# Longer DMA runs for keys, wq and values, with a set-aside quarter, in a decode step of attention and a gated feed-forward layer

## The chip, the cores and the metric

The kernel runs on 1 core of one Trainium2 chip. A core has five engines that run side by side: TensorE (PE) for matrix products, VectorE (DVE), ScalarE (ACT), GpSimd (POOL), and SyncE (SP), which here only issues transfers. Sixteen DMA engines move data from memory (HBM) into the on-chip buffers. The metric is device time in microseconds (us), lower is better. Before the change it is 696.13 us, the median of 3 runs (696.13 to 696.16).

## The reference

One token (x, 512 numbers) goes through an attention block with a long cache and through a gated feed-forward layer; a scalar gate mixes the two results.

```python
def _A_ref(x, k_cache, v_cache, wq, wo):       # Hq, Dh = 32, 128; 8 KV heads, Sk = 32768
    q = (x @ wq).reshape(B, Sq, Hq, Dh).transpose(0, 2, 1, 3)
    k, v = jnp.repeat(k_cache, 4, axis=1), jnp.repeat(v_cache, 4, axis=1)
    p = softmax(einsum("bhqd,bhkd->bhqk", q, k) * Dh ** -0.5)
    o = einsum("bhqk,bhkd->bhqd", p, v)
    return o.transpose(0, 2, 1, 3).reshape(B, Sq, Hq * Dh) @ wo

def _B_ref(x, w1, w3, w2):                     # D, F = 512, 1792
    return (silu(x @ w1) * (x @ w3)) @ w2

g = sigmoid((x * gate_w).sum(-1, keepdims=True))
return g * _A_ref(...) + (1 - g) * _B_ref(...)
```

All is float32. The keys are 134 MB, the values as many; wq and wo have 8.4 MB each, w1, w2 and w3 3.7 MB each: 296 MB in all, each byte read once.

## The kernel before

**Tiles and units.** Two tiles of 64 KB in each of the 128 partitions, `big_a` and `big_b`, take turns for nearly everything that is loaded. Each has two halves, `region(b, z)`, with the dependency names A0, A1, B0, B1. A *key unit* t (0 to 15) is 8.4 MB: a quarter of the keys of a pair of KV heads. It comes as two loads, one per half (`load_keys`, L331), and in each of them a partition gets a run of 32 KB. A *value unit* s (0 to 15) is half a head's values, 8.4 MB; units 0 to 11 come as one load with runs of 64 KB into `big_b` (`load_values`, L409). The values lag the keys by four units (`LAG`).

**What is done with a unit.** For each half of a key unit DVE makes four chunks: a block transpose of 128x2048 into `kt0` or `kt1` in turn (L355). PE multiplies each chunk with a small window of queries (L344; ScalarE copies the window into `winc`, L338) and adds up in PSUM. Behind the eighth chunk ScalarE copies the scores out (L361) and PE clears the bank (L244). After each fourth unit PE turns the scores (`turn`, L374, instructions on L371), and DVE with ScalarE makes the softmax of that pair (L378: maximum L381, subtraction L393, exponent L398, sums L403). A value unit is multiplied by its weights in 32 products (`values_all`, L430, with the weights copied by ScalarE on L418), and DVE takes the useful blocks out (`own`, L440, with L442 and L446).

**Order.** The instruction order of every engine is the order in which the program adds operations; each engine works through its list and waits on semaphores. SyncE has one list of loads, each of which waits until the readers of its target are done. The semaphore on which a transpose tells that it is done is counted down by the PE product that uses it, so a load that overwrites keys waits for PE's product on the last chunk read from its half. In the loop over units (L453) a step adds: scores of unit t, the next keys' loads, and for t of 4 and more the value product of unit t - 4, then the next values' load. The softmax of four units stands one unit later, behind the scores of unit t + 1, and `turn` at the end of the step t = 3, 7, 11, 15. PE's part of this is written as three nested loops (L661 to L676), with a branch that leaves out the values in the first four units.

**Start.** SyncE loads wq in two halves into `big_a` (x between them), then w1 and w3 into `big_b`, then keys 0 into `big_a`, keys 1 into `big_b`, 2 into a, 3 into b, and all later keys into a. PE makes the queries (L270), ScalarE and DVE lay them into `win` (L288 to L298); then come the hidden products of w1 and w3 (L307), the sigmoid (L313) and three DVE steps (L314, L316, L320).

**End.** Values 12 (two halves), wo (quarters of 2.1 MB in `wo_t`, a tile that nothing else uses), 13, 14 (two halves) and 15 (in three pieces), then w2 in five pieces into `big_a`. DVE multiplies wo's rows into `acc` (`mix`, L525); the last products close the sum and ScalarE's queue writes 2 KB out.

Of the kernel before, what the change touches and what calls it, by code (L numbers as in the profile page):

```python
# [116 lines left out]
def kernel(  # L117
# [79 lines left out]
    wqd = wq.rearrange("(p c) n -> p (c n)", c=NC)  # L197
    for z in range(2):
        load(region(0, z), wqd[:, z * R:(z + 1) * R], [f"A{z}"])
        if z == 0:  # L200
            load(rows[0][0:1, :], x.rearrange("a b n -> (a b) n"), ["row0"])
            pr.add("ACT", lambda: nc.scalar.dma_start(rows[1][0:1, :], gate_w.rearrange("(o n) -> o n", o=1)),
                   writes=["row1"], inc="gate", by=16)
    for z, t in enumerate((w1, w3)):
        load(region(1, z)[:, 0:NC * F], t.rearrange("(p c) f -> p (c f)", c=NC), [f"B{z}"])
# [6 lines left out]
    mt, mtt = sbuf("mt", 32), sbuf("mtt", 32)  # L212
# [47 lines left out]
    pe(columns, reads=["row0", "ident"], writes=["m0"])  # L260
# [3 lines left out]
    for c in range(NC):  # L264
        def part(c=c):
            t = region(0, c // 2)
            for b in range(2):
                for j in range(4):
                    o = ((c % 2) * HKV + 4 * b + j) * REP * DH
                    ins = T.matmul(  # L270
                        pf[b][32 * j:32 * j + 32, :], xp[:, c, :], t[:, o:o + REP * DH],
                        start=(c == 0), stop=(c == NC - 1),
                    )
            return ins
        pe(part, reads=[f"A{c // 2}", "xp"], writes=["f0", "f1"])
# [25 lines left out]
    for z in range(2):  # L301
        def ff(z=z):
            t = region(1, z)
            for c in range(NC):
                for j in range(4):
                    o = c * F + FJ * j
                    ins = T.matmul(  # L307
                        pf[2 + z][32 * j:32 * j + 32, 0:FJ], xp[:, c, :], t[:, o:o + FJ],
                        start=(c == 0), stop=(c == NC - 1),
                    )  # L310
            return ins
        pe(ff, reads=[f"B{z}", "xp"], writes=[f"f{2 + z}"])
    act(lambda: A.activation(silu[:, 0:FJ], pf[2][:, 0:FJ], AF.Sigmoid), reads=["f2"], writes=["silu0"])  # L313
    dve(lambda: V.tensor_mul(silu[:, 0:FJ], silu[:, 0:FJ], pf[2][:, 0:FJ]), reads=["f2", "silu0"], writes=["tmp0"])  # L314

    dve(lambda: V.scalar_tensor_tensor(  # L316
        rows[0][:, 0:FJ].rearrange("p (k a) -> p k a", k=FR), silu[:, 0:FJ].rearrange("p (a k) -> p k a", k=FR),
        gate[:, 1:2], pf[3][:, 0:FJ].rearrange("p (a k) -> p k a", k=FR), op0=ALU.mult, op1=ALU.mult,
    ), reads=["tmp0", "gate1", "f3"], writes=["row0"])
    dve(lambda: V.transpose(htp.rearrange("p k a -> p (k a)"), rows[0][:, 0:FJ]), reads=["row0"], writes=["htp"])  # L320

    kd = k_cache.rearrange("a (w u) s d -> w (a u s d)", u=2).rearrange("w (p m z r) -> w m z p r", p=P, m=4, z=2)
    vd = v_cache.rearrange("a h (e p n) d -> (a h) e p (n d)", e=2, p=P)

    def where(t):
        return 1 if t in (1, 3) else 0

    def load_keys(t):  # L331
        b = where(t)
        for z in range(2):
            load(region(b, z), kd[t // 4, t % 4, z], ["AB"[b] + str(z)])
# [15 lines left out]
    def scores(t, z, win_op):  # L350
        kin = region(where(t), z).rearrange("p (n c j) -> p c n j", c=4, j=32)
        key = "AB"[where(t)] + str(z)
        for c in range(4):
            dst = kt[c % 2].rearrange("p (n i) -> p n i", i=32)
            k = dve(lambda c=c, d=dst: V.transpose(d, kin[:, c]), reads=[key], writes=[f"kt{c % 2}"], credit="keys")  # L355
# [18 lines left out]
    def turn():  # L374
        for f in range(4):
            pe(lambda f=f: turn_part(f), reads=[("sb", m) for m in range(4)] + ["ident"], writes=[f"f{f}"], loop=True)

    def softmax(w):  # L378
# [17 lines left out]
        ), reads=["top"], writes=banks)  # L396
        for u in range(2):
# [4 lines left out]
            ), reads=banks, writes=[("prob", u)])  # L402
# [46 lines left out]

    load_keys(0)  # L450
    vals = {}
    first = window(0, 0)
    for t in range(NH):  # L453
        v = t - LAG
        scores(t, 0, first)
        second = window(t, 1)
        if v >= 1:
            own(v - 1)
            if v % 4:
                vals[v] = (vals[v], weights(v))  # L460
        scores(t, 1, second)
        scores_out(t)
        if t + 1 < NH:
            load_keys(t + 1)
            first = window(t + 1, 0)

        if v >= 0 and v % 4 == 0:
            softmax(v // 4)
            vals[v] = (vals[v], weights(v))
        if v >= 0:  # L470
            values_loop(*vals.pop(v))
        if v + 1 >= 0 and t + 1 < NH:
            vals[v + 1] = load_values(v + 1)
        if t % 4 == 3:
            turn()
# [83 lines left out]
    def load_halves(s):  # L559
        for z in range(2):  # L560
            load(region(0, z), vd[s // 2, s % 2][:, z * R:z * R + R], [f"A{z}"])

    load_halves(12)
    load_wo(0)
    load(big[1], vd[6, 1], ["B0", "B1"])
    own(11)
    softmax(3)
# [7 lines left out]
    load_halves(14)  # L575
# [59 lines left out]
    for a, b in parts[2:]:  # L635
        ff_down([(htp[:, k, :], w2t[:, k, :], k == 8, k == FR - 1) for k in range(a, b)], reads=["htp", ("w2", a)])
        if a == 8:
# [4 lines left out]
           reads=["res"], inc="out", by=16)  # L642
# [5 lines left out]
    a = next(i for i, o in enumerate(ops) if o.loop)  # L648
    b = max(i for i, o in enumerate(ops) if o.loop) + 1
    assert all(o.loop for o in ops[a:b])  # L650
    pr.emit("PE", ops[:a])
    half = T.alloc_register("half")
    T.reg_mov(half, 0)
# [5 lines left out]


    with nc.Fori(0, NP, 1, engines=[PE], head_slot={PE: 0}):  # L661
# [46 lines left out]
```

## Time and profile before

| | |
|---|---|
| median of the runs | 696.13 us |
| the profiled execution: its time, its span | 695.86 us, 694.0 us |
| granted TensorE clock, mean | 0.774 |
| PE, DVE, ACT busy | 402.1, 376.2, 45.3 us |
| bytes read from HBM, mean rate | 296.23 MB, 427 GB/s |
| L355, 128 transposes of 128x2048 | 2287 ns each |
| L344, 1024 products of scores | 186.1 us in all |
| L430, 768 products of values | 110.2 us in all |

The span goes from the first to the last instruction of the program. "Busy" counts neither waiting nor issuing. A page cuts the span into 40 equal slices and gives each one's busy share in tenths. A line of the timeline has the start, the length, engine, line and operation, the tiles written and read, how many instructions are taken together, and in brackets how long the engine had been idle and what ended that. In the waits, a line has the total time, the number of waits and the longest. "PEq" is PE's sequencer, "SPq" SyncE's.

### The profile page before, as it was taken

How to read it: one execution, taken by the hardware profiler on the slowest of the kernel's cores; microseconds unless marked ns; L12 is line 12 of the kernel's file. 1: busy time of each engine (PE TensorE's matmuls, PEld its weight loads, DVE VectorE, ACT ScalarE, POOL GpSimd, SP SyncE). 2: the span in 40 equal slices, each digit the busy share in tenths (PEclk: the TensorE clock that was granted, in tenths of full speed). 3: DMA queues.
4: the chain of work that ended last, by engine and by line, in shares of the span. 5: the costliest groups of instructions: out<-in, count | busy, mean ns of one | idle time of the engine just before them, and what ended most of it. 6: DMA issues, size and time to landing. Idle time of an engine off the chain costs nothing. (4 is left out here: it accounts for less than half of the span.)

```text
span 694.0 us, 5676 instructions
## 1 busy us (share of the span) xinstructions
PE 402.1 (58%) x2400; PEld 92.6 (13%) x2400; DVE 376.2 (54%) x263; ACT 45.3 (7%) x90; POOL 2.6 (0%) x15
## 2 busy tenths in 40 slices
PE   3636566647556554746667644538456555376756
PEld 1100001101010110201010101201010101131112
DVE  1029999885719081686619091786529090654121
ACT  0200000020100000010100000020100000100000
POOL 1000000000000000000000000000000000000000
PEclk9966877877887796867665898977876776777679
DMA  9999999999999999999999999999999999999996
GB/s 391 421 425 444 431 425 433 467 399 427 451 419 431 444 448 404 450 423 427 465 406 448 416 442 419 442 431 450 427 423 434 419 472 399 447 425 424 427 422 285
DMA packets 9380, 296.34 MB, mean 427 GB/s; under 512 B 1046, under 2 KB 1050, under 8 KB 1436
## 3 DMA queue, kind: packets, MB, share of 16 engines
q1 hardware_dynamic: 9362, 296.23, 99.2%
q8 instruction: 5, 0.08, 0.0%
q14 instruction: 3, 0.02, 0.0%
q10 hardware_dynamic: 10, 0.00, 0.0%
HBM read 296.23 MB, written 0.00 MB: 427 GB/s over the span
## 5 line engine op out<-in xcount | busy, mean ns | idle before, releaser
L355 DVE STREAM_TRANSPOSE kt<-big_a 128x2048 f32<-128x2048 f32 x112 | 250.2, 2287 | 182.3 <-DMA big_a<-in_A_k_cache_dram 180.8
L344 PE MATMUL ps<-kt,winc 128*32 128x512 f32 x1024 | 186.1, 807 | 132.7 <-PEq L658 132.7
L430 PE MATMUL ps<-big_b,pv 128*32 128x512 f32 x768 | 110.2, 738 | 74.0 <-PEq L658 74.0
L344 PEld LDWEIGHTS ps<-kt,winc 128*32 128x32 f32 x1024 | 26.5, 122 | 287.0 <-issue 287.0
L430 PEld LDWEIGHTS ps<-big_b,pv 128*32 128x32 f32 x768 | 30.3, 132 | 153.7 <-issue 153.7
L355 DVE STREAM_TRANSPOSE kt<-big_b 128x2048 f32<-128x2048 f32 x16 | 35.7, 2287 | 3.2 <-DMA big_b<-in_A_k_cache_dram 3.2
L527 DVE SCALAR_TENSOR_TENSOR acc<-wo_t,own_rows,acc 128x512 f32<-128x512 f32 x24 | 18.0, 752 | 28.2 <-DMA wo_t<-in_A_wo_dram 27.4
L244 PE MATMUL ps<-acc 128*128 128x512 f32 x34 | 20.5, 687 | 21.8 <-PEq L658 20.3
L338 ACT COPY winc<-win 128x128 f32<-128x128 f32 x32 | 9.8, 307 | 341.9 <-PE ps L344 341.9
L540 PE MATMUL ps<-big_b,probs 128*32 128x512 f32 x128 | 19.4, 767 | 14.2 <-DMA big_b<-in_A_v_cache_dram 14.2
L361 ACT COPY sb<-ps 128x512 f32<-128x512 f32 x16 | 17.0, 1063 | 151.3 <-PE ps L344 151.3
L540 PE MATMUL ps<-big_a,probs 128*32 128x512 f32 x128 | 20.7, 811 | 5.1 <-DMA big_a<-in_A_v_cache_dram 5.1
L403 DVE TENSOR_REDUCE sums<-probs 128x8 f32<-128x2048 f32 x4 | 15.3, 3822 | 8.0 <-ACT probs L398 8.0
L442 DVE TENSOR_TENSOR tmp<-ps,own_b 128x512 f32<-128x512 f32 x12 | 7.9, 655 | 20.1 <-PE ps L430 20.1
L307 PE MATMUL turned<-big_b,xp 128*32 128x448 f32 x64 | 9.2, 734 | 9.6 <-DMA big_b<-in_B_w_dram 9.6
L270 PE MATMUL turned<-big_a,xp 128*32 128x512 f32 x64 | 11.7, 902 | 2.7 <-DMA big_a<-in_A_wq_dram 2.4
L446 DVE TENSOR_REDUCE red<-tmp 128x128 f32<-128x1024 f32 x6 | 11.5, 1915 | 0.2
L244 PEld LDWEIGHTS ps<-acc 128*128 128x128 f32 x34 | 5.4, 201 | 39.1 <-issue 37.6
L398 ACT ACTIVATE probs<-turned 128x1024 f32<-128x1024 f32 x8 | 7.8, 1021 | 38.5 <-DVE turned L393 38.5
L393 DVE TENSOR_TENSOR turned<-turned,top 128x2048 f32<-128x2048 f32 x4 | 9.2, 2300 | 0.1
L381 DVE TENSOR_REDUCE mt<-turned 128x8 f32<-128x2048 f32 x4 | 9.0, 2260 | 0.0
L549 DVE TENSOR_SCALAR red<-ps,own_b 128x128 f32<-128x128 f32 x2 | 0.7, 348 | 15.3 <-PE ps L540 15.3
(80 smaller groups left out, 95.7 us busy)
## 6 DMA issues: line engine op xcount, KB each, us to landing
big_a<-in_A_k_cache_dram SPq DMA_DIRECT2D x28, 4096.0 KB, 28.3
big_b<-in_A_k_cache_dram SPq DMA_DIRECT2D x4, 4096.0 KB, 30.7
big_a<-in_A_v_cache_dram SPq DMA_DIRECT2D x4, 4096.0 KB, 27.7
big_a<-in_A_wq_dram SPq DMA_DIRECT2D x2, 4096.0 KB, 16.4
wo_t<-in_A_wo_dram SPq DMA_DIRECT2D x4, 2048.0 KB, 18.0
big_b<-in_B_w_dram SPq DMA_DIRECT2D x2, 3584.0 KB, 33.7
big_b<-in_A_v_cache_dram SPq DMA_DIRECT2D x1, 4096.0 KB, 27.3
big_b<-in_A_v_cache_dram SPq DMA_DIRECT2D x2, 2048.0 KB, 34.0
```

Of the source, the lines that this page charges most:

```text
L244: return T.matmul(ps_s, acc[:, 0:P], acc, start=True, stop=False, skip_group_check=True)
L270: ins = T.matmul(pf[b][32 * j:32 * j + 32, :], xp[:, c, :], t[:, o:o + REP * DH], start=(c == 0), stop=(c == NC - 1),)
L307: ins = T.matmul(pf[2 + z][32 * j:32 * j + 32, 0:FJ], xp[:, c, :], t[:, o:o + FJ], start=(c == 0), stop=(c == NC - 1),)
L338: lambda: A.copy(winc, win[:, t // 4, :, 16 - 16 * z:48 - 16 * z]),
L344: ins = T.matmul(ps_s[32 * g:32 * g + 32, :], winc[:, c, :], kt[c % 2][:, 512 * g:512 * g + 512], start=False, stop=False, skip_group_chec ...
L355: k = dve(lambda c=c, d=dst: V.transpose(d, kin[:, c]), reads=[key], writes=[f"kt{c % 2}"], credit="keys")
L361: lambda: A.copy(sb[:, :, :, t % 4], ps_s.rearrange("p (n i) -> p n i", i=32)),
L403: dve(lambda: V.tensor_reduce(sums[:, 8 * w:8 * w + 8].rearrange("p (u q) -> p u q", u=2), probs[:, :, 0:1024].rearrange("p u (n q) -> p u ...
L430: ins = T.matmul(ps_o[32 * t:32 * t + 32, :], pv[:, o:o + 32], big[1][:, n * P:(n + 4) * P], start=((z, g) == (0, 0)), stop=((z, g) == (1, ...
L446: dve(lambda: V.tensor_reduce(red[h], tmp.rearrange("p e b d -> p d (e b)"), axis=AX.X, op=ALU.add), reads=["tmp0", "tmp1"], writes=[("red ...
L527: dve(lambda k=k: V.scalar_tensor_tensor(acc, wo_t[:, k, :], own_rows[:, w, k:k + 1], acc, op0=ALU.mult, op1=ALU.add,), reads=["wo", ("own ...
L540: ins = T.matmul(ps_o[32 * t:32 * t + 32, :], prob[u][:, o:o + 32], vt[:, n * P:(n + 4) * P], start=((e, z, g) == (0, 0, 0)), stop=((e, z, ...
```

## The change

Keys are loaded as one load per unit with runs of 64 KB, and so are wq and value units 12 and 14 (unit 15 stays in three pieces). As soon as a key unit has landed, ScalarE copies the quarter that the last two chunks of the second half need (128x4096) into `wo_t` (`set_aside`); those two transposes read it there, so the next load into the tile waits for six transposes and that copy. Key units 0 and 2 go to `big_b`, 1 and 3 to `big_a`. w1 and w3 are loaded behind key unit 3, into `big_b`, and the hidden products and the three DVE steps stand behind the fourth unit's `turn` and softmax; they use the PSUM banks `pm` in place of `pf`. x and gate_w are both issued by ScalarE. `turn` now stands ahead of the value product, and the softmax in the same step as `turn`. An instruction ahead of the exponent writes a one-column tile `mark`. PE has two loops, of 4 and of 12 units, with `turn` and the hidden products written out between them.

```diff
-    wqd = wq.rearrange("(p c) n -> p (c n)", c=NC)
-    for z in range(2):
-        load(region(0, z), wqd[:, z * R:(z + 1) * R], [f"A{z}"])
-        if z == 0:
-            load(rows[0][0:1, :], x.rearrange("a b n -> (a b) n"), ["row0"])
-            pr.add("ACT", lambda: nc.scalar.dma_start(rows[1][0:1, :], gate_w.rearrange("(o n) -> o n", o=1)),
-                   writes=["row1"], inc="gate", by=16)
-    for z, t in enumerate((w1, w3)):
-        load(region(1, z)[:, 0:NC * F], t.rearrange("(p c) f -> p (c f)", c=NC), [f"B{z}"])
+    for i, t in enumerate((x.rearrange("a b n -> (a b) n"), gate_w.rearrange("(o n) -> o n", o=1))):
+        pr.add("ACT", lambda i=i, t=t: nc.scalar.dma_start(rows[i][0:1, :], t), writes=[f"row{i}"], inc="row", by=16)
+    load(big[0], wq.rearrange("(p c) n -> p (c n)", c=NC), ["A0", "A1"])
...
-        pe(part, reads=[f"A{c // 2}", "xp"], writes=["f0", "f1"])
+        pe(part, reads=["A0", "A1", "xp"], writes=["f0", "f1"])
...
-    kd = k_cache.rearrange("a (w u) s d -> w (a u s d)", u=2).rearrange("w (p m z r) -> w m z p r", p=P, m=4, z=2)
+    kd = k_cache.rearrange("a (w u) s d -> w (a u s d)", u=2).rearrange("w (p m r) -> w m p r", p=P, m=4)
     def where(t):
-        return 1 if t in (1, 3) else 0
+        return 1 if t in (0, 2) else 0
     def load_keys(t):
         b = where(t)
-        for z in range(2):
-            load(region(b, z), kd[t // 4, t % 4, z], ["AB"[b] + str(z)])
+        load(big[b], kd[t // 4, t % 4], ["AB"[b] + str(z) for z in range(2)])
+    spare = wo_t.rearrange("p k e -> p (k e)").rearrange("p (n r) -> p n r", n=NB)
+    def set_aside(t):
+        src = region(where(t), 1).rearrange("p (n r) -> p n r", n=NB)[:, :, 64:128]
+        act(lambda: A.copy(spare, src), reads=["AB"[where(t)] + "1"], writes=["wo"])
...
         for c in range(4):
+            src, key = kin[:, c], "AB"[where(t)] + str(z)
+            if (z, c) >= (1, 2):
+                src, key = spare[:, :, 32 * (c - 2):32 * (c - 2) + 32], "wo"
             dst = kt[c % 2].rearrange("p (n i) -> p n i", i=32)
-            k = dve(lambda c=c, d=dst: V.transpose(d, kin[:, c]), reads=[key], writes=[f"kt{c % 2}"], credit="keys")
+            k = dve(lambda d=dst, s=src: V.transpose(d, s), reads=[key], writes=[f"kt{c % 2}"], credit="keys")
...
+        act(lambda: A.copy(mark, ones[:, 0:1]), reads=["ones"], writes=["mark"])
         for u in range(2):
             act(lambda u=u: A.activation(
...
-            ), reads=banks, writes=[("prob", u)])
+            ), reads=[*banks, "mark"], writes=[("prob", u)])
...
     for t in range(NH):
         v = t - LAG
+        set_aside(t)
         scores(t, 0, first)
-        second = window(t, 1)
-        if v >= 1:
-            own(v - 1)
-            if v % 4:
-                vals[v] = (vals[v], weights(v))
-        scores(t, 1, second)
+        scores(t, 1, window(t, 1))
         scores_out(t)
+        if t == LAG - 1:
+            load_hidden()
         if t + 1 < NH:
             load_keys(t + 1)
             first = window(t + 1, 0)
-        if v >= 0 and v % 4 == 0:
-            softmax(v // 4)
-            vals[v] = (vals[v], weights(v))
+        if v >= 1:
+            own(v - 1)
+        if t % 4 == 3:
+            turn(v >= 0)
         if v >= 0:
-            values_loop(*vals.pop(v))
+            values_loop(vals.pop(v), weights(v))
+        if t == LAG - 1:
+            hidden_products()
         if v + 1 >= 0 and t + 1 < NH:
             vals[v + 1] = load_values(v + 1)
         if t % 4 == 3:
-            turn()
+            softmax(t // 4)
+        if t == LAG - 1:
+            hidden()
...
-    load_halves(12)
+    load_unit(0, 12)
     load_wo(0)
-    load(big[1], vd[6, 1], ["B0", "B1"])
+    load_unit(1, 13)
     own(11)
-    softmax(3)
...
-    load_halves(14)
+    load_unit(0, 14)
...
+    def unit():
+        with nc.Fori(0, 2, 1, engines=[PE]):
+            take("windows")
+            for c in range(4):
+                take("keys")
+                scores_part(c).then_inc(done, 1)
+        take("scores")
+        zeros().then_inc(done, 1)
+    with nc.Fori(0, LAG, 1, engines=[PE], head_slot={PE: 0}):
+        unit()
+    pr.emit("PE", ops[b:c])
+    left = T.alloc_register("left")
+    T.reg_mov(left, 4)
+    with nc.Fori(0, NH - LAG, 1, engines=[PE], head_slot={PE: 0}):
+        unit()
+        T.reg_sub(left, left, 1)
+        with T.If_cmp(left, 0, "IS_EQ"):
+            for f in range(4):
+                turn_part(f).then_inc(done, 1)
+            T.reg_mov(left, 4)
+        take("values", 16)
+        take("weights")
+        values_all().then_inc(done, 1)
+    pr.emit("PE", ops[d:])
```

`load_hidden`, `hidden_products` and `hidden` hold the lines of before (L204, L301 to L320) with `pm[z]` in place of `pf[2 + z]`; `load_unit(b, s)` loads a whole value unit into `big[b]`.

## The prediction

> **What bounds the kernel now.** I read the page first, then the busy shares by stretch, then SyncE's waits, then the timeline of one period, and last the packet records.
>
> ```profile
> span 694.0 us, 5676 instructions
> ...
> DMA  9999999999999999999999999999999999999996
> ...
> q1 hardware_dynamic: 9362, 296.23, 99.2%
> ```
>
> The reader is to see that one queue, SyncE's, keeps the 16 DMA engines busy 99.2% of the span, in every slice but the last.
>
> ```profile
> 40.00:136.00 96.00, 59.26 (x328) 11.26 (x328) 79.48 (x37) 5.93 (x12) 0.00 (x0) 0.79 1.01 433
> 136.00:582.00 446.00, 257.28 (x1512) 54.55 (x1512) 254.41 (x152) 30.73 (x54) 0.00 (x0) 0.76 1.00 433
> ```
>
> The last three columns are granted clock, DMA share and GB/s. The share is full in the stretch of key units alone and in that of keys and values in turn, while PE and DVE idle for much of the second. So the time is the time of the packets, plus 1.93 us ahead of the first one and 3.65 us behind the last landing (690.31). A faster engine brings nothing; a gain needs cheaper packets, and a loss needs a queue that runs dry.
>
> The packet records give the price of a packet, by size (count, bytes, mean ns):
>
> ```
> 4992  32768  1219.1
> 1664  65536  2422.1
> ```
>
> The 32 KB packets are the keys (32 loads of 128), wq (256), values 12 and 14 (512) and half of value 15 (128). They take 1213 ns for wq, 1217 for keys between 55 and 120 us, 1221 for value 12: the price goes with the length of the run, not with the tensor. Two of 32 KB take 2438.2, one of 64 KB 2422.1.
>
> How far ahead the queue is fed shows in one period.
>
> ```profile
> SPq L191 <- PE ps L344: 303.7, 30, 13.5
> SPq L413 <- PE ps L430: 191.6, 11, 18.9
> ```
> ```profile
> 177.09 8.95 DVE L355 STREAM_TRANSPOSE kt<-big_a 128x2048 f32<-128x2048 f32 x4 [0.25 <-DMA big_a<-in_A_k_cache_dram]
> 178.39 9.24 SPq L191 DMA_DIRECT2D big_a<-in_A_k_cache_dram  x2
> ...
> 186.19 1.06 PE L344 MATMUL ps<-kt,winc 128*32 128x512 f32 x8 [1.13 <-PEq L658]
> ```
>
> A key load is released by the score product of the last chunk read from its half: the half that landed at 176.99 is transposed from 177.09 to 186.04, its last product ends at 187.25 and the next half's load is issued at 187.30, some 15 us before its data can start. Values are issued about 7 us ahead. That spare time is what the change may spend.
>
> **The change, part by part.** L is the landing of a unit on the slowest engine.
>
> *Longer runs.* 4864 packets of 32 KB (keys, wq, values 12 and 14) become 2432 of 64 KB: 2432 x 16.1 ns / 16 engines = 2.45 us less. There are 19 loads fewer, each with one 9 ns semaphore write per engine: 0.17 us. Bounds: 0.4 us if only wq and the values gain and keys for some reason do not; 2.6 whole. I take 2.6, as a 32 KB packet costs the same from all three sources.
>
> The Trainium skill (DMA: Bandwidth & Descriptors, "Why small descriptors are slow") puts the fixed cost of a packet at about three cycles; at the 850 MHz that the page gives for the fabric this would be, as an estimate, 3.5 ns, a saving of 0.5 us and a time of some 696.0 with the stall below. The records show 16.1 ns, so I go by them.
>
> *One load for a whole unit.* The next key load now waits for six transposes (instead of four, per half) and for ScalarE's copy. Six take 13.35 (a row of six at 134.23 took 13.34), the product starts 0.15 later and takes 1.06 at full clock or 1.94 at half, the issue follows 0.05 later: release at L + 14.7 to 15.6. Meanwhile a value unit of 19.35 us (landings 176.99 to 196.34) is on the engines. From SP's first issue (0.93) to the first packet (1.93) passed 1.0 us, and the first packets took some 0.6 longer than later ones, so the queue stays full if the issue comes by L + 17.85 to 18.25. Margin 2.2 or more: nothing lost. Without it each of the 12 loads from key 5 to value 12 would lose the excess.
>
> *ScalarE's copy of 128x4096.* No row shows one. From below: L418's slope against L338, (614 - 307)/384 = 0.8 ns an element, 3.5 us; from above, L361 from PSUM against L338, (1063 - 307)/384 = 2.0, 8.4 us. I take 4 us (nearest: L398, 1021 ns for 1024). Either end is done before the sixth transpose, 13.4 us after the landing. Behind it on ScalarE waits the second window, wanted 11 us after the landing; so even 8.4 costs nothing by itself. The last two transposes read wo_t, which is ready; the first wo load then waits for the eighth product, at L + 20, and its data start near L + 38.
>
> *wq whole, x by ScalarE.* All 64 query products now start when wq is down (22.4): 2 x 5.34 to 2 x 6.39, then 6.0 to the first window (27.89 to 33.85): 39.1 to 41.2. Key 0 lands at 22.4 + 19.4 = 41.8. Hidden; key 1 is issued at 33 to 36, wanted at 40.7.
>
> *Key units alone (0 to 3).* Eight transposes are 17.8 per 19.37 us: DVE keeps up. Behind key 3 come w1 and w3, 17.0 us (twice 22.27 to 30.77), so key 4 has to be issued by L + 15.5 to 15.9, and is released at 14.7 to 15.6: nothing to 0.1.
>
> *Softmax and hidden products behind unit 3.* Here it gets tight.
>
> ```profile
> 129.10 1.08 ACT L361 COPY sb<-ps 128x512 f32<-128x512 f32 x1 [8.91 <-PE ps L344]
> ...
> 131.25 1.91 PE L371 MATMUL turned<-ident,sb 128*128 128x128 f32 x16
> ...
> 147.49 2.25 DVE L381 TENSOR_REDUCE mt<-turned 128x8 f32<-128x2048 f32 x1
> ...
> 150.01 1.28 ACT L398 ACT_TABLE_LOAD   x1
> ...
> 154.42 1.94 ACT L398 ACTIVATE probs<-turned 128x1024 f32<-128x1024 f32 x2 [3.12 <-DVE turned L393]
> ...
> 156.39 3.82 DVE L403 TENSOR_REDUCE sums<-probs 128x8 f32<-128x2048 f32 x1 [2.00 <-ACT probs L398]
> ```
>
> Transposes end at L + 17.9, the product at 19.1 (20.0 at half clock), turn 4.06 after the copy out starts (129.10 to 133.16): 23.2 to 25. Maximum to subtraction 6.9, then a table load of 1.28, which in the new order waits for DVE (before, it lay beside it), exponent 1.94, sums 3.8, and the three DVE steps of the hidden layer, 2.3 (L314, L316, L320): 39.6 to 41.5. Key 4 lands at 17.0 + 19.4 = L + 36.4, so DVE takes it up 3.2 to 5.1 late and key 5 is released 17.9 to 20.6 after that landing, wanted by 17.85 to 18.25. Loss 0 at full clock, up to 2.7 at half; the mean granted clock is 0.77, and only one or two of the products on this chain fall in a half-clock stretch. I take 0.6. Value 0 waits for the hidden products, 6.4 (all at full clock) to 12 us behind the turn: L + 30 to 37, wanted at 35: nothing, at most 2.
>
> *Later softmaxes.* No hidden layer, and a table load in one of three: DVE is free at L + 36.9 to 40.1 where the next keys land at 38.7: at most 1.4 late, inside the margin of 2.2. Turn ahead of the value product moves this to an end at L + 32 to 36; the next values are wanted at 37.6.
>
> *The end.* In the last stretch value 12 and 14 land whole; their products are done some 10 us after, and the next loads of those buffers start 14 us or more after. The last wo and w2 pieces are as before. Nothing.
>
> *Instruction fetches.* The records show 16 KB packets of an instruction queue among the data (34.9, 47.3, 598.8, ...), and from the first of them one engine lands 1.8 us after the first of the sixteen, where it had been 0.3; that lag stays to the end. PE's stream is cut anew, so this may fall away or hit one engine twice: -1.5 to +1.5, taken as 0. A queue that ran dry would also level the engines, so that a later fetch is paid again.
>
> Sum: 694.0 - 2.6 + 0.6 = 692.0 of span. The profiled execution took 695.86 for its span of 694.0, and the median of the runs is 0.27 above it; 2.1 on top gives 694.1.
>
> **The rivals.**
>
> *Stall behind unit 3.* The half-clock end of the chain: 2.7 for key 5, with 1.5 for a fetch paid again: 693.5 + 1.2 to 4.2 = 694.8 to 697.7. For it: DVE has all of softmax and the hidden layer ahead of key 4. Against: clock stretches are 3 to 10 us and alternate, so the whole chain is hardly at half.
>
> *The gain is not there*, keys staying at their old rate: 696.1 - 0.4 + 0.6 = 696.3. Against: values in runs of 32 and of 64 KB show the price on one tensor. By the Trainium skill's three cycles (above) it would be 696.0.
>
> *Slower: the copy slows the transposes.* ScalarE and DVE read the same tile at once, in each of 16 units. If DVE ran at half speed for 8.4 us it would lose 4.2, the release would move to 18.9 to 19.8, 0.7 to 1.6 late, times 12 loads = 8 to 19, and the key-only stretch (22 us of DVE per 19.4) some 8 more: 710 to 721. It decides from a lengthening of 2.2 a unit on, and is over 0.2% slower from about 3. Against: at 178.40 and 178.60 ScalarE copies lie inside the four transposes of 177.09, which take 8.95 like those at 167.31 with 8.96; but those copies are short.
>
> **How the numbers follow.** No change can be told within 0.2%, 694.74 to 697.52. Forecast (saving whole, stalls below 1.2, a fetch more or less): 692.0 to 694.7, 0.66. Stall behind unit 3: 0.20, of it 0.01 above 697.52. No gain: 0.05. Slower by the copy, or by another release late in every period: 0.09. So faster 0.66, same 0.24, slower 0.10. The likeliest case alone is 692.6 to 694.7; the range goes to 692.0 for a fetch that falls away and to 697.6 for the stall.
>
> **What would show it.** Packets of 32 KB down to 128, those of 64 KB at 2422 ns for keys; 16.1 ns a pair. Each key load issued 14.7 to 15.6 after the landing before it. The copy near 4 us, six transposes still 13.4. DVE's first transpose of key 4 some 3 to 5 us after its landing, and if anywhere, DMA idle at that value's end. A DMA share below 0.99 in each value's stretch would prove me wrong, and so would key packets over 2430 ns.

## The result, and the profile after

The changed kernel takes 700.0 us (median of 11 runs, 698.02 to 705.2), the one before 696.15 (11 runs, 695.94 to 696.4): a ratio of 1.0066, 95% interval 1.0045 to 1.0086 (here and below the ratio compares the means of the runs, so it can differ a little from that of the medians). It is slower by 0.66% where 694.1 was forecast. Its times also spread over 7 us where those of before spread over 0.5. The profiled execution took 699.78 for a span of 697.7.

The page of the changed kernel (instructions; DMA by slice; the queue's packets, MB and share of 16 engines; then groups: count, busy time, mean ns, idle time before them):

```profile
span 697.7 us, 5701 instructions
...
DMA  9999999999999999999999999999999999999996
...
q1 hardware_dynamic: 6624, 296.23, 98.9%
...
L336 DVE STREAM_TRANSPOSE kt<-big_a 128x2048 f32<-128x2048 f32 x84 | 187.1, 2285 | 182.0 <-DMA big_a<-in_A_k_cache_dram 182.0
...
L313 ACT COPY wo_t<-big_a 128x4096 f32<-128x4096 f32 x14 | 50.5, 3606 | 174.0 <-DMA big_a<-in_A_k_cache_dram 174.0
```

The new copy costs ScalarE 3.6 us a unit, the transposes take 2285 ns as before (2287), and the queue has 29% fewer packets. The DMA digits are the same as before, all 9 but the last. Nothing here says where 3.7 us of span came from. The busy shares by stretch (the last columns are granted clock, DMA share and GB/s) say more, for the changed kernel:

```profile
82.00:102.00 20.00, 10.91 (x66) 1.84 (x66) 17.66 (x8) 5.65 (x5) 0.00 (x0) 0.91 0.95 406
...
119.00:141.00 22.00, 10.54 (x94) 4.28 (x90) 12.84 (x18) 6.76 (x9) 0.00 (x0) 0.89 0.95 407
40.00:136.00 96.00, 55.03 (x344) 11.35 (x344) 77.84 (x46) 23.64 (x21) 0.00 (x0) 0.86 0.98 417
136.00:582.00 446.00, 239.56 (x1502) 50.03 (x1502) 250.12 (x141) 72.23 (x66) 0.00 (x0) 0.77 1.00 432
```

From 40 to 136 us the rate fell from 433 to 417 GB/s, and two stretches, those in which keys 3 and keys 4 come in, have 406 and 407. A slice of the page is 17.4 us wide, and its 9 stands for anything from 90% on. The share itself is a poor witness, because a packet that takes longer than it should counts as busy all the while. So the landings were read one by one: a load has landed when the last of the 16 engines has written its semaphore, and two loads without a disturbance land 19.34 to 19.39 us apart per 8.4 MB in runs of 64 KB (22 such pairs here, most of them at 19.35 or 19.36) and 9.71 per 4.2 MB in runs of 32 KB (37 pairs in the trace of before). These are the key loads of the changed kernel that came later than that. "Ahead" is how long before the landing of the load in front of it a load was issued; all times in us.

```
load      issued   ahead   landed   interval   late by
keys 3     78.37    4.00   102.28     19.91      0.56
keys 4    117.71    1.56   140.51     21.25      1.89
keys 5    156.12    3.78   179.38     19.48      0.13
keys 6    194.01    4.71   218.20     19.48      0.13
keys 7    233.70    3.86   257.63     20.07      0.72
keys 12   427.88    3.97   451.56     19.71      0.36
keys 15   544.46    3.85   568.70     20.39      1.04
```

They make 4.8 us together. The other key loads of the period were issued 4.65 to 4.72 ahead and lost 0.05 at most. Keys 0 lost 1.55 to an instruction fetch (a 16 KB packet at 34.53), as w3 did in the trace of before (1.50, packet at 34.87). The balance of the two traces: the last of all landings moved from 690.31 to 694.08, by 3.77. Of that, +0.16 is wq, +4.71 what loads lost against undisturbed intervals (6.74 now, 2.03 before), and -1.10 what is left, the gain of the longer runs. Behind the last landing nothing changed (3.65 before, 3.63 after).

SyncE's waits in the changed kernel (us in all, times, longest) answer to those of before:

```profile
SPq L191 <- PE ps L323: 191.4, 18, 14.5
...
SPq L396 <- PE ps L413: 162.1, 11, 16.1
```

They look alike: that SyncE waits for a product is the design in both. What counts is how long before the end of the queued work that wait is over, and this view doesn't hold it. The timeline of keys 3 does:

```profile
102.30 13.28 DVE L336 STREAM_TRANSPOSE kt<-big_a 128x2048 f32<-128x2048 f32 x6 [2.25 <-DMA big_a<-in_A_k_cache_dram]
102.38 3.61 ACT L313 COPY wo_t<-big_a 128x4096 f32<-128x4096 f32 x1
...
115.50 4.53 DVE L336 STREAM_TRANSPOSE kt<-wo_t 128x2048 f32<-128x2048 f32 x2
...
115.72 1.94 PE L323 MATMUL ps<-kt,winc 128*32 128x512 f32 x8 [1.13 <-PEq L667]
117.71 0.33 SPq L191 DMA_DIRECT2D big_a<-in_A_k_cache_dram  x1
...
140.54 3.61 ACT L313 COPY wo_t<-big_a 128x4096 f32<-128x4096 f32 x1 [3.05 <-DMA big_a<-in_A_k_cache_dram]
...
141.55 13.30 DVE L336 STREAM_TRANSPOSE kt<-big_a 128x2048 f32<-128x2048 f32 x6
```

Keys 3 landed at 102.28, six transposes and a product at half clock (1.94, at a granted clock of 0.50; the same product took 1.06 at 1.00) later keys 4 were issued, 15.43 after the landing. The load in front, w3, reported its end from its sixteen engines between 117.55 and 119.27, so for the first of them the issue came too late altogether. Keys 4 then landed 1.89 late and pushed everything behind them.

### The profile page after: what moved, and what is told of

The parts are those of the page before. It is cut to its first block, busy times and chain, and to the rows that moved or that the text cites. A ratio compares the mean times of both kernels' runs of the same rounds, so it can differ in the third digit from the quotient of the medians.

```text
span 697.7 us, 5701 instructions
## 1 busy us (share of the span) xinstructions
PE 374.9 (54%) x2400; PEld 87.9 (13%) x2400; DVE 374.6 (54%) x263; ACT 105.5 (15%) x112; POOL 2.6 (0%) x15
## 5 line engine op out<-in xcount | busy, mean ns | idle before, releaser
L323 PE MATMUL ps<-kt,winc 128*32 128x512 f32 x1024 | 182.7, 792 | 238.7 <-PEq L667 238.7
L336 DVE STREAM_TRANSPOSE kt<-big_a 128x2048 f32<-128x2048 f32 x84 | 187.1, 2285 | 182.0 <-DMA big_a<-in_A_k_cache_dram 182.0
L413 PE MATMUL ps<-big_b,pv 128*32 128x512 f32 x768 | 89.3, 619 | 0.0
L313 ACT COPY wo_t<-big_a 128x4096 f32<-128x4096 f32 x14 | 50.5, 3606 | 174.0 <-DMA big_a<-in_A_k_cache_dram 174.0
L336 DVE STREAM_TRANSPOSE kt<-wo_t 128x2048 f32<-128x2048 f32 x32 | 71.6, 2274 | 0.0
L239 PE MATMUL ps<-acc 128*128 128x512 f32 x34 | 26.3, 866 | 21.8 <-PEq L667 20.3
L342 ACT COPY sb<-ps 128x512 f32<-128x512 f32 x16 | 17.1, 1067 | 135.1 <-PE ps L323 135.1
L336 DVE STREAM_TRANSPOSE kt<-big_b 128x2048 f32<-128x2048 f32 x12 | 26.7, 2284 | 11.1 <-DMA big_b<-in_A_k_cache_dram 11.1
L413 PEld LDWEIGHTS ps<-big_b,pv 128*32 128x32 f32 x768 | 23.8, 114 | 65.6 <-issue 65.6
L265 PE MATMUL turned<-big_a,xp 128*32 128x512 f32 x64 | 9.0, 725 | 11.9 <-DMA big_a<-in_A_wq_dram 11.9
L352 PEld LDWEIGHTS turned<-ident,sb 128*128 128x128 f32 x64 | 9.3, 169 | 3.3 <-issue 3.3
```

Of the source, the lines that this page charges most:

```text
L239: return T.matmul(ps_s, acc[:, 0:P], acc, start=True, stop=False, skip_group_check=True)
L313: act(lambda: A.copy(spare, src), reads=["AB"[where(t)] + "1"], writes=["wo"])
L323: ins = T.matmul(ps_s[32 * g:32 * g + 32, :], winc[:, c, :], kt[c % 2][:, 512 * g:512 * g + 512], start=False, stop=False, skip_group_chec ...
L336: k = dve(lambda d=dst, s=src: V.transpose(d, s), reads=[key], writes=[f"kt{c % 2}"], credit="keys")
L342: lambda: A.copy(sb[:, :, :, t % 4], ps_s.rearrange("p (n i) -> p n i", i=32)),
L352: ins = T.transpose(pf[f][:, P * a:P * a + P], sb[:, 4 * f + a].rearrange("p i m -> p (i m)"), ident)
```

## The experiments

Two theories stood against each other. A: keys are issued too close to the end of the queued work, and the time goes in the first packets of such loads, whatever their length. B: the run length is at fault, a queue of 64 KB packets being refilled worse than one of 32 KB; as the texts below put it, the lead needed is two packets' time, 4.84 us at 64 KB and 2.4 at 32 KB. The C of those texts is that the long runs or the copy cost time by themselves, at any lead. The rival of the prediction, that the copy slows the transposes, had fallen with the 2285 ns above. All medians below stand beside 696.09 to 696.15 of the kernel before.

**Release by the transpose.** The sixth transpose tells the load by a tiny DVE copy behind it, in place of the product that reads its result.

```diff
...
+            if (z, c) == (1, 1):
+                names = ["AB"[where(t)] + str(y) for y in range(2)]
+                read = dve(lambda: V.tensor_copy(told, ones[:, 0:1]), reads=["ones", *names])
+                for n in names:
+                    pr.readers[n] = [r for r in pr.readers[n] if r.eng != "DVE"] + [read]
```

> The changed kernel, but the next key load waits for the sixth transpose itself (a tiny DVE copy behind it tells that it is read) instead of for the product on it: release at L + 13.6 whatever the clock, not L + 14.6 to 15.6. Theory A (late issue: a load issued under some 4.7 us ahead of the slowest landing before it has long first packets, and all 4.7 us that the changed kernel lost lie there): every key load of the period regains its loss, lead 5.7; key 4 (17.0 us of w1 and w3 ahead of it) keeps a lead of 3.4 and loses 0.5; key 5 has DVE late by 2.7 or more and loses 0.5 to 1.9. Span 694.0 to 695.7, time 696 to 698, runs closer together than 698 to 705. Theory C (the 64 KB runs of the keys, or the copy beside the transposes, cost by themselves): 700 as before.

Measured: 699.44 (697.32 to 700.33, 4 runs), ratio 1.0037 (1.0022 to 1.0051); slower than expected. The period's key loads were issued 5.9 ahead, and none of them lost more than 0.1; that part went by A. (Value 12, also 5.9 ahead, lost 0.5.) Keys 4 (1.37 ahead) lost 2.26 and keys 5 (0.29 ahead) 2.38, for reasons that the timeline of this kernel shows:

```profile
104.33 2.04 PE L239 MATMUL ps<-acc 128*128 128x512 f32 x2 [1.28 <-PEq L672]
...
108.12 8.89 DVE L336 STREAM_TRANSPOSE kt<-big_a 128x2048 f32<-128x2048 f32 x4 [2.15 <-PE ps L323]
...
139.64 3.81 DVE L391 TENSOR_REDUCE sums<-probs 128x8 f32<-128x2048 f32 x1 [3.34 <-ACT probs L386]
...
145.60 13.30 DVE L336 STREAM_TRANSPOSE kt<-big_a 128x2048 f32<-128x2048 f32 x6
158.82 0.11 DVE L341 COPY told<-ones 128x1 f32<-128x1 f32 x1
```

The clear of the bank on PE ran at a granted clock of 0.50 (2.04 for two products, where the changed kernel's trace has 1.10 at 1.00), so DVE idled 2.15 for a free `kt`; and at keys 4, which landed at 140.06, DVE was 5.5 late, still busy with softmax and the hidden layer. In this trace each half-clock product in the wrong place, and each late start of DVE, comes out of the lead of the next load.

**One chunk set aside, not two.** The opposite: seven transposes before the release, about 2.2 us less lead in every unit.

```diff
-        src = region(where(t), 1).rearrange("p (n r) -> p n r", n=NB)[:, :, 64:128]
-        act(lambda: A.copy(spare, src), reads=["AB"[where(t)] + "1"], writes=["wo"])
+        src = region(where(t), 1).rearrange("p (n r) -> p n r", n=NB)[:, :, 96:128]
+        act(lambda: A.copy(spare[:, :, 32:64], src), reads=["AB"[where(t)] + "1"], writes=["wo"])
...
-            if (z, c) >= (1, 2):
+            if (z, c) >= (1, 3):
```

> The changed kernel with only the last chunk set aside (128x2048), so that a load waits for seven transposes: release at L + 16.9 to 17.8, lead 2.5 to 1.6 us. Theories A and B: each of the 14 key loads and value 12 now loses 0.6 to 1.9 us, key 4 some 4: span 708 to 722, time 710 to 724. Theory C (runs or copy, not the issue): about 700, or less, as the copy is half as long.

Measured: 721.96 (2 runs), ratio 1.0371 (1.0353 to 1.0389). Ten loads (nine of keys, and value 12), issued 0.05 to 2.75 ahead, lost 1.1 to 3.7 each, 26.1 together. Four more, issued 2.5 to 2.85 ahead, lost 0.15 or less: a short lead makes a loss likely, it doesn't fix its size. The stretch of the period shows it in the rate, 414 where before had 433:

```profile
136.00:582.00 446.00, 228.99 (x1462) 47.80 (x1462) 237.05 (x135) 51.84 (x67) 0.00 (x0) 0.77 0.97 414
```

**Three chunks set aside, release by the fifth transpose.** ScalarE also copies the second chunk of the second half (128x2048, 1.90) into a tile `more`; room comes from small tiles that share memory.

```diff
...
+        act(lambda: A.copy(more, src[:, :, 32:64]), reads=["AB"[where(t)] + "1"], writes=["more"])
         act(lambda: A.copy(spare, src[:, :, 64:128]), reads=["AB"[where(t)] + "1"], writes=["wo"])
...
+            if (z, c) == (1, 1):
+                src, key = more, "more"
...
+            if (z, c) == (1, 0):
+                names = ["AB"[where(t)] + str(y) for y in range(2)]
+                read = dve(lambda: V.tensor_copy(told, ones[:, 0:1]), reads=["ones", *names])
...
```

> The changed kernel with three chunks set aside (128x2048 more, in a tile of its own; three small tiles share others' room for it) and the load released by the fifth transpose itself: release at L + 11.4, lead 8 us, for key 4 5.6. Theories A and B: no long first packets but at key 5, where DVE is 3.2 to 5.1 late (lead 4.8 to 2.9): loss 0 to 0.8. Span 692.5 to 693.5, time 694.6 to 695.6, faster than before by 0.1 to 0.2%, runs within 1 us. Theory C: 700, or more as the copy is longer.

Measured: 695.87 (695.4 to 698.59, 12 runs), ratio 1.0006 (0.9998 to 1.0015). 4.1 us came back. Seven of twelve runs have a span of 693.5 to 693.9, the others 695.1 to 696.7. In the profiled one keys 4, issued 5.85 ahead, lost 0.24, and no key load behind them lost more than 0.1.

**Runs of 32 KB, at the time of the changed kernel.** This is the test of B. A key unit comes in two loads again, one per half, and the first try was this:

```diff
...
-        load(big[b], kd[t // 4, t % 4], ["AB"[b] + str(z) for z in range(2)])
+        for z in range(2):
+            load(region(b, z), kd[t // 4, t % 4, z], ["AB"[b] + str(z)], over=["AB"[b] + str(1 - z)])
```

> The changed kernel with each key unit as two loads of 32 KB runs, both behind the same wait as the one load, so issued as late. Theory A (a load needs some 4.7 us of lead whatever its runs): the same losses at the same loads, 4.7 us, plus 1.3 for the shorter runs: 701. Theory B (an engine holds two packets, so the lead needed is two packets' time, 4.84 us at 64 KB and 2.4 at 32 KB): losses nearly gone, only key 4 with its lead of 1.6 keeps 0.5 to 1; span 694 to 695, time 696 to 697. Theory C: with 64 KB runs as the cause 694 to 695 too, but then with no long first packets at key 4.

Measured: 735.88 (4 runs, ratio 1.0574, 1.0558 to 1.0589), far from either forecast, because in this form the second load also waits until the first has landed. So it says nothing on A and B. It measures another thing instead, the price of a queue that is dry: a second load, issued 0.02 us after the landing, lands some 12.1 later (12.04 to 12.17) instead of 9.71, 2.3 to 2.5 more. The next version issues both halves together:

```diff
+        for z in range(2):
+            load(region(b, z), kd[t // 4, t % 4, z], ["AB"[b] + str(z)], over=["AB"[b] + "1"] if z == 0 else [])
```

> What e2 was meant to be: the changed kernel with each key unit as two loads of 32 KB runs, issued one behind the other at the moment when the changed kernel issues its one load (the second waits for nothing more). Theory A (some 4.7 us of lead whatever the runs): long first packets wherever the release came with a product at half clock, losses of 3 to 5 us as in the changed kernel, and 1.3 for the shorter runs: 700 to 702. Theory B (the lead needed is two packets' time, 2.4 us at 32 KB): no long first packets at leads over 2.5, key 4 alone (lead 1.6) loses 0.5 to 1: span 694.5 to 695.5, time 696.5 to 697.5, runs closer together.

Measured: 695.95 (10 runs, ratio 0.9998, 0.9989 to 1.0007). This doesn't decide either: DVE began when the first half had landed, so all but keys 5 (4.78) were issued 8.6 us or more ahead again, and at such leads A and B foretell the same. In the third version the first transpose waits for both halves:

```diff
-            k = dve(lambda d=dst, s=src: V.transpose(d, s), reads=[key], writes=[f"kt{c % 2}"], credit="keys")
+            k = dve(lambda d=dst, s=src: V.transpose(d, s), reads=[key, "AB"[where(t)] + "1"] if (z, c) == (0, 0) else [key], writes=[f"kt{c % 2}"], credit="keys")
```

> The changed kernel with each key unit as two loads of 32 KB runs, issued one behind the other at the same late moment; the transposes of a unit now wait until both have landed (in e2b they began with the first half, which made the issue early again). Theory A (an engine's first packet is long when its lead is under some 3.5 us, whatever the runs): the leads of the changed kernel and so its losses, 3 to 5 us, plus 1.4 for the shorter runs: span 698 to 701, time 700 to 703. Theory B (two packets' time: 2.4 us at 32 KB): only leads under 2.4 cost; key 4 loses some 1.9, the rest under 1 in all: span 696 to 697.5, time 698 to 699.5.

Measured: 702.04 (700.71 to 702.58, 4 runs), ratio 1.0083 (1.0068 to 1.0099). Runs of 32 KB that are issued as late as those of 64 KB lose as much: the 2 us above 700.0 hold the 1.1 that short runs cost by themselves (last experiment), and the rest is inside the spread. The landings say it load by load: three key loads issued 3.28, 3.85 and 3.86 ahead landed 1.88, 0.48 and 1.15 late, where by B a lead of 2.4 is enough, and those issued 4.66 ahead or more lost nothing. Theory B falls.

**The hidden layer's DVE steps later.** On top of the three chunks, the steps L314, L316 and L320 of before stand behind the transposes of unit 4, out of the way of keys 4.

```diff
...
+        if t == LAG:
+            hidden()
...
-            hidden()
```

> The kernel with three chunks set aside, and the three DVE steps of the hidden layer moved behind the transposes of key unit 4. If the runs of 695 to 696.7 span of that kernel come from key 5 (DVE late at key 4), they go: all runs at 693.3 to 694 span, time 695.3 to 696. If they come from key 4 (DVE waits at the start of key 3 while PE clears the bank at half clock), some 3 to 5 of 12 runs stay 1 to 3 us above the rest.

Measured: 695.77 (695.5 to 697.57, 11 runs), ratio 1.0001 (0.9992 to 1.001): no difference to three chunks alone that 0.1% can show. Two of the eleven runs still lie 1.8 above the median, so DVE's lateness at keys 4 wasn't what made the slow runs.

**A fourth chunk for the first four units.** While no softmax has run, `probs` is free, and, on top of the last version, units 0 to 3 put one more chunk there; their loads then wait for four transposes.

```diff
...
+        if t < LAG:
+            act(lambda: A.copy(early, src[:, :, 0:32]), reads=["AB"[where(t)] + "1"], writes=["early"], over=["pad0", "pad1"])
...
-            if (z, c) == (1, 0):
+            if (z, c) == ((0, 3) if t < LAG else (1, 0)):
```

> That kernel with a fourth chunk set aside in key units 0 to 3 (128x2048 into the tile that holds the exponents later), so that these loads are released by the fourth transpose: key 4 at L + 9.1 to 11.3, wanted by 12.3. With both late loads gone every run is at 693.3 to 694.0 span, 695.3 to 695.9, all within 0.8 us, faster than before by 0.05 to 0.1%: the longer runs give 1.4 and a fetch or two takes some back. If runs still spread by over 1.5 us, the cause of the spread is not a late key load.

Measured: 695.66 (695.47 to 696.55, 11 runs), ratio 0.9996 (0.9986 to 1.0005). The times near 697 and 698 of the two versions above no longer come up. The same place in the timeline, and the same stretch, of this kernel:

```profile
101.43 8.89 DVE L346 STREAM_TRANSPOSE kt<-big_a 128x2048 f32<-128x2048 f32 x4 [1.59 <-DMA big_a<-in_A_k_cache_dram]
110.25 0.11 DVE L351 COPY told<-ones 128x1 f32<-128x1 f32 x1
```

```profile
110.39 0.33 SPq L191 DMA_DIRECT2D big_a<-in_A_k_cache_dram  x1
```

```profile
40.00:136.00 96.00, 50.15 (x344) 11.30 (x344) 78.75 (x50) 38.92 (x29) 0.16 (x2) 0.91 1.01 435
```

Keys 4 are issued 7.3 us earlier than in the changed kernel, and the rate is 435 instead of 417. No key or value load is issued less than 5.8 us ahead. This version keeps all other parts of the change, so they aren't what cost the time. It is the best by its median, and not faster than the kernel before by more than the interval.

**Only the start early.** Units 0 to 3 as in the last version, the period as in the changed kernel, release by the product behind the sixth transpose. The lines stand against the last version.

```diff
...
         if t < LAG:
             act(lambda: A.copy(early, src[:, :, 0:32]), reads=["AB"[where(t)] + "1"], writes=["early"], over=["pad0", "pad1"])
-        act(lambda: A.copy(more, src[:, :, 32:64]), reads=["AB"[where(t)] + "1"], writes=["more"])
+            act(lambda: A.copy(more, src[:, :, 32:64]), reads=["AB"[where(t)] + "1"], writes=["more"])
...
-            if (z, c) == ((0, 3) if t < LAG else (1, 0)):
+            if t < LAG and (z, c) == (0, 3):
```

> The changed kernel with key units 0 to 3 alone released early (four chunks aside, by the fourth transpose itself) and the hidden layer's DVE steps behind unit 4; units 4 to 15 as in the changed kernel, released by the sixth chunk's product. This parts the loss of 4.7 us into start and period: key 3, 4 and 5 (2.6 us) come back, the period's 2.1 stay and vary with the clock of that product. Span 694.5 to 696.5, time 696.5 to 698.5, between e1 and e8. If it is as fast as e8, the period lost nothing; if it is at 699 or more, the start was not the larger part.

Measured: 698.98 (695.46 to 701.43, 10 runs), ratio 1.0031 (1.0015 to 1.0048), more than expected. By the medians the early start is worth 1.0 us (700.0 to 698.98) and an early period 3.3 (698.98 to 695.66). The start loses nothing now but the fetch; six loads of the period lose 6.2 in the profiled run (701.43, the longest of the ten). Its largest is keys 5:

```profile
136.78 3.81 DVE L401 TENSOR_REDUCE sums<-probs 128x8 f32<-128x2048 f32 x1 [3.34 <-ACT probs L396]
140.50 13.40 DVE L346 STREAM_TRANSPOSE kt<-big_a 128x2048 f32<-128x2048 f32 x6
```

```profile
155.16 0.33 SPq L191 DMA_DIRECT2D big_a<-in_A_k_cache_dram  x1
```

Keys 4 landed at 138.07 and DVE took them up 2.4 late, behind the sums. Keys 5 were issued 17.1 after that landing and 2.25 ahead, and lost 2.16. Keys 7 (3.87 ahead) lost 1.58, while keys 11 with the same lead (3.86) lost nothing.

**The early version with runs of 32 KB.** What the longer runs bring: two loads a unit, issued together, in the version with the fourth chunk; the first transpose waits for both halves.

```diff
...
-        load(big[b], kd[t // 4, t % 4], ["AB"[b] + str(z) for z in range(2)])
+        for z in range(2):
+            load(region(b, z), kd[t // 4, t % 4, z], ["AB"[b] + str(z)], over=["AB"[b] + "1"] if z == 0 else [])
...
-            k = dve(lambda d=dst, s=src: V.transpose(d, s), reads=[key], writes=[f"kt{c % 2}"], credit="keys")
+            k = dve(lambda d=dst, s=src: V.transpose(d, s), reads=[key, "AB"[where(t)] + "1"] if (z, c) == (0, 0) else [key], writes=[f"kt{c % 2}"], credit="keys")
```

> e8 (all loads early) with the keys in two loads of 32 KB runs, issued together: the worth of the long runs alone, with no late load in either. By the prediction's price (16.1 ns a pair of packets) it is 2.06 us above e8; by the landings of before and after (9.71 for 4.2 MB, 19.35 for 8.4) 16 x 0.075 = 1.2 us: span 694.7 to 695.1, time 696.7 to 697.1.

Measured: 696.79 (696.59 to 697.15, 11 runs), ratio 1.001 (1.0001 to 1.0019). Against 695.66 with runs of 64 KB, the long runs of the 16 key units are worth 1.1 us (1.4 by the last landings of the two profiled executions, 691.55 and 690.12; of these some 0.4 are late landings and wq, which differ between the two). This version is 0.7 above the kernel before, whose key runs it shares: its last landing is 1.24 later, 0.13 of it with wq, the rest because more loads landed late (1.3 at the first keys, 0.9 at value 13, 0.5 at value 7, against 1.5 at w3 before). So of the 1.1 us of cheaper runs the best version has only 0.4 to 0.5 left by its median.

## Why the prediction was wrong

**The step that failed: "the queue stays full if the issue comes by L + 17.85 to 18.25".** It took the 1.0 us from the kernel's first issue to its first packet, and 0.6 for the first packets' extra length, for the lead that a load needs. The issues came when they were foretold (L + 14.7 to 15.6; measured in the period 14.6 to 15.6), and many of the loads behind them were late. By all 64 KB key and value loads of seven traces but keys 0 (the changed kernel, the two with one and three chunks aside, the one with the `told` copy, and the three later ones in long runs):

```
issued ahead of the           loads   late by, mean   largest
landing in front, us
0 to 1                           2        3.04          3.70
1 to 2                           6        2.52          3.38
2 to 3                          10        1.39          3.01
3.7 to 4.2                       9        0.66          1.58
4.2 to 5                        19        0.04          0.68
5 and more                     164        0.05          0.99 (at an instruction fetch)
```

In the rows from 2 to 4.2 some loads lost nothing. So the margin of "2.2 or more" was none: a key load of the period is issued 3.85 to 4.7 ahead, at the edge, and a product at half clock (1.94 for 1.06) decides which side it falls on. That fits the spread of the changed kernel's times, 7 us, where the version without late loads spreads over 1.1. In the kernel before the keys were issued 16.5 to 19.0 ahead in the period and values 9.1 to 10.7 ("some 15" and "about 7" in the prediction), so no row of it could show what a lead of 4 costs.

Two things were missing. The first is the spread over engines. From keys 0 on the first of the 16 ended each load 1.5 to 2.1 us before the last (2.5 at keys 15), and the landing shows some 0.4 after the last packet: keys 4.0 ahead of a landing (keys 3) were only 1.7 to 3.5 ahead of the engines' own ends. The second is that the load lands with the worst of 16, and the delay has a tail; an engine that ended early can lose some time before it is the worst, which fits that some short leads cost nothing. The trace doesn't name a packet's engine, so first packets were matched by time to the engine end before them (3225 of 3360 could be; where several engines stood idle together the pairing is a guess, so the largest values are uncertain). The delay of a first packet against undisturbed 2.42 was:

```
this engine's lead, us   packets   mean delay   largest
under -1                     30        3.50        4.61
-1 to 0                      92        2.19        2.98
0 to 1                      100        1.36        2.31
1 to 2                      131        0.95        3.43
2 to 3                      222        0.26        2.46
3 to 4                      197        0.10        1.98
4 to 5                      252        0.02        0.72
5 and more                 2201        0.01        0.54
```

At keys 15 of the changed kernel the leads are 1.8 to 3.4; fourteen engines lost 0.4 at most, two had first packets of 3.54 and 3.79, and the unit was 1.04 late. The Trainium skill (DMA: Bandwidth & Descriptors, "Why a DMA increments its semaphore by 16 and not by 1") says that the sixteen finish independently and that only the full count means landed; the traces agree, by this unit.

For an engine that has run dry, the time from issue to data is near what was assumed: lead and delay add up to 1.66 on average for leads below -0.5 (72 packets), against 1.0 + 0.6. The error lies in taking that as enough for an engine that hasn't.

**The mis-sized term: the saving, "I take 2.6".** It measured 1.1 to 1.3: landings go from 2 x 9.71 to 19.35 or 19.36, 0.06 to 0.07 a unit, times 19 units; and 1.1 by the last experiment. The packet records misled in two ways. Neighbouring records on an engine overlap by 3 to 4 ns, and two short packets hold that overlap twice. And the mean of 1219.1 holds packets that were disturbed in that one execution: in the version with early loads and short runs 32 KB packets start 1213.6 apart on average, undisturbed 64 KB ones of before 2418.6, so a pair of short ones costs some 8.6 ns more and not 16.1. Intervals between landings have neither fault. The rate of the Trainium skill's three cycles per packet (DMA: Bandwidth & Descriptors, "Why small descriptors are slow") would have given, as an estimate, 0.5; the 1.1 lies between that and my 2.6.

Together: 2.6 - 1.1 = 1.5 from the saving, 4.7 - 0.6 = 4.1 from late loads, 0.2 from wq, make 5.8, against 5.7 between the span of 692.0 that was summed up and 697.7.

**Right:** the release times. Six transposes in 13.3, the copy in 3.6 (4 was taken), its rival (710 to 721) without a trace. Value 0, issued 9.0 ahead, lost 0.03. Keys 0 and 1 and the end cost nothing new. Fetches: 1.55 for 1.50.

**Half right:** the rival "stall behind unit 3" (694.8 to 697.7) named the place, keys 4 and 5, and the mechanism, DVE late behind the softmax; in the `told` version keys 5 lost 2.4 in this way, near the 2.7 that was worked out. In the changed kernel's own trace the loss fell on keys 4 instead ("nothing to 0.1", measured 1.89), which made DVE's lateness there only 1.0. **"Inside the margin of 2.2"** for later softmaxes was wrong with the margin itself, and a slower rival by "another release late in every period" was given too little: it comes nearest to what happened. "Clock stretches are 3 to 10 us" was short as well: in the trace of before they are 3.4 to 23.9.

Of the two signs that were to prove the forecast wrong, one came: the 64 KB packets took 2438 ns on average, those of the keys alone some 2448, over the 2430 that was named. The other didn't: the share in the stretch where values come in, 136 to 582, stayed at 1.00, and only that from 40 to 136, mostly keys, fell to 0.98.

**Open.** Why an engine that still has one whole packet in hand gets its next one late, now and then by 2 us or more, isn't settled; no run varied what the engines do between issue and first packet. That lead, and not run length, brings the loss is shown (by the versions with more lead, with less, and with short runs at the same lead); what the queue does with that lead is not.

## What to carry to other kernels

Where a kernel is bound by one queue, "the DMA share is full" doesn't say how near the queue is to running dry: list for every load how long before the end of the load in front it is issued, for the slowest engine and for the fastest, and look at what comes under 4 to 5 us. A change that merges loads to save packets also merges their releases; price the saving by intervals between landings, and the lead it spends by the worst of sixteen engines. If the time of a version spreads by 1% where its neighbour's spreads by 0.1%, look for a load at that edge; here there was one.

## What the hardware showed that was not expected

A dry queue cost 2.3 to 2.5 us each time (32 KB runs, issued 0.02 after the landing), and part of such a loss stands in lengthened packets, which count as busy (at the changed kernel's keys 4 the first packets took 2.5 to 3.2 in place of 2.42). The Trainium skill (DMA: Bandwidth & Descriptors, "Latency and other measured facts") gives about 0.6 us from a queue's issue to its first byte; the trace has 1.0 at the kernel's start, of which the issuing instruction itself is 0.38 and what follows it 0.6, as the page has it; for dry engines in mid-kernel it has 1.66 on average, counted from the start of the issue and with the lengthening of the first packet. The memory latency in the same section, 0.2 us on average and 2 at high load, would fit the longer one, but no run here separates memory from the queue.

One 16 KB packet of an instruction queue among the data made the load after wq 0.9 to 1.55 us late (in the long-run traces, and 1.50 a load later in that of before), because one engine in sixteen then lags and the load waits for it; one later fetch, at 634 in the early version, took 1.0 again, while those at 133 and 597 cost nothing that its landings show. ScalarE read a tile that DVE was transposing for 3.6 to 7.4 us a unit, and the transposes out of that tile kept their 2280 to 2290 ns (2287 before).
